# Loading k whole and first, then q by halves, for the first pair of heads of a bucketed attention with a rational feed-forward layer

## The chip, the cores and the metric

The kernel runs on 1 core of one Trainium2 chip. The metric is the device time of one execution in microseconds (us). The profile is of one execution; PE is TensorE (PEld its weight loads), DVE is VectorE, ACT is ScalarE, POOL is GpSimd, SP is SyncE, which here only issues transfers.

## The reference

Attention in which a query sees only the keys of its own bucket (six sign bits of a projection), then a feed-forward layer with a rational activation. Cut to what matters here:

```python
q_bits = (np.einsum('bhsd,dk->bhsk', q, proj) > 0).astype(np.int64)
k_bits = (np.einsum('bhsd,dk->bhsk', k, proj) > 0).astype(np.int64)
mask = q_bucket[:, :, :, None] == k_bucket[:, :, None, :]
scores = scale * np.matmul(q, k.transpose(0, 1, 3, 2))
scores = np.where(mask, scores, -1000000000.0)
scores = scores - np.max(scores, axis=-1, keepdims=True)
attn = np.exp(scores)
attn = attn / (np.sum(attn, axis=-1, keepdims=True) + 1e-09)
...
x = np.ascontiguousarray(attn_out.transpose(0, 2, 1, 3)).reshape(B * S, H * D)
h = x @ w_in
P = a[0] + a[1] * h + a[2] * h2 + a[3] * h3
Q = 1.0 + np.abs(b[0]) * np.abs(h) + np.abs(b[1]) * h2
return ((P / (Q + 1e-6)) @ w_out).astype(np.float32)
```

There are 4 batches of 8 heads, 768 tokens and 64 numbers per head; the layer has 3072 tokens, 512 by 2048 by 512.

## The kernel before, in words

The 32 heads are worked on as 16 pairs, numbered p. A pair's `qT[p]` and `kT[p]` are 128 by 768: one head's 64 rows above the other's, the tokens along the free dimension. Each operand is split into a high part of shorter format (`high`, a cast on ACT, tiles `q` and `k` of the profile) and a low part (`low`, a subtraction, tiles `lo`), and transfers and copies arrange high and low parts in `Q1`, `K1`, `Q2`, `K2`. Rows 64 and up of `Q1` and `K1` hold the bits of the buckets as penalties, so that one product gives the masked score.

For each pair, 12 steps of `maxstep` (two matmuls into `psm`, one DVE reduce to a column of `m`) find the maximum of each query row over all keys. The maxima go as a row into `Q1` (`shift_turn`, `shift_rows`; for pair 0 `first_shift`: three small matmuls into `pst`, then one DVE operation). Then 12 steps of `scores` (for each head two matmuls into `pss` and an exponential on ACT into `E`, with sums on POOL into `acc`) and 12 of `values` (`psv`). After the 16 pairs the layer runs, `psh` and `pso` in the profile.

Every engine executes in the order in which the program issues (lines 70 to 91), so an instruction that waits holds back all that stands behind it on its engine or queue. That order comes from a plan: `at(p, s, f)` (line 471) enters an action under the number 12p + s, and lines 582 to 584 issue them by rising number. The numbers in `FIRST` (lines 50 to 60) place the actions of pairs 0, 1 and 2; `MID` and `LAST` place the others. Before the plan comes a fixed list for pair 0 (lines 531 to 549).

Pair 0 has functions of its own, since nothing hides its start. `first_bits(t)` (line 294) projects q (t = 0) or k (t = 1) in two halves of 384 tokens into `psb_first`; `first_compare(t, hf)` (304) turns a half into bits on DVE; `first_penalties(h, hf)` (310) scales q's bits into `Q1` on ACT; `first_cross(t)` (314) copies the second head's rows down on ACT; `first_k_rows` (318) copies k's bit rows for the other head on POOL; `first_second_high` (321) makes four more copies on ACT; `second_low` (222) issues four transfers of the low parts on SP. `first_shift(hf, h)` (326) makes the row of maxima for one head and half. `warm(n)` (186) issues n matmuls on zeros, `psw`, whose result nobody reads. `maxstep` and `first_shift` share two PSUM buffers (`psa`).

The first actions of the plan, in order, are `maxstep` 0, 2, 1, 7, 6 of pair 0, `first_shift(0, 0)`, `maxstep` 8, two half `scores`, `first_compare(0, 1)`, `first_shift(0, 1)`, the bits of pair 1 (`second_bits`, `psb`, and two compares), four more half `scores`, and `maxstep` 4, 5, 9, 10. Steps 0 to 2 and 6 to 8 need only the first 384 tokens of q, but all of k.

Of the kernel before, what the change touches and what calls it, by code (L numbers as in the profile page):

```python
# [7 lines left out]
F32 = mybir.dt.float32  # L8
F32R = mybir.dt.float32r
# [4 lines left out]
ALU = mybir.AluOpType  # L14
# [4 lines left out]
P = 128  # L19
S = 768  # L20
HQ = 384
# [20 lines left out]
    group=6, values=[0.66, 0.05], values_out=3.5, maxima=7.17,  # L42
    maxima_steps=[0, 1.15, 1.73, 2.64, 3.32, 5.08, 5.86, 6.98, 8.0, 8.84, 10.26, 11.37], sums=14.65, sums_store=17.37,
    high=[-0.41, 1.19], low=[1.06, 3.35], bits=2.81, penalties=4.05, high_move=1.9, maskrows=5.61, second_low=-2.2,
    second_high=2.69, load_v=10.99, shift_turn=8.61, shift_rows=8.82, load=9.0, recips=[20.0, 22.0, 23.0],
    weights=[[1.44, 4.0, 4.1, 5.09, 5.49, 7.11, 9.5, 9.75, 17.5], [8.05, 10, 10.65, 11.5, 12.38, 14.29, 16.34, 19.32, 21.22]],
# [1 line left out]
)  # L48

FIRST = dict(  # L50
    maxima1=4.62, rate1=0.45, maxima2=9.5, rate2=0.82, high=[3.25, 3.53], low=[6.0, 7.3], bits=7.15, penalties=7.25,
    high_move=4.53, maskrows=8.2, second_low=4.25, second_high=4.35, load_v=4.78, group=2,
    values=[2.35, 2.65, 2.32, 2.35, 0.35, 0.61], values_out=3.02, high1=[-0.27, -5.58], low1=[11.24, 4.95],
    high_move1=20.05, load2=21.89, load3=-1.5, penalties1=-6.57, maskrows1=3.69,
    weights=[[-5.7, 6.64, 6.7, 11.42, 12.19, 18.75, 21.75, 38.77, 44.13], [8.03, 9.04, 9.24, 11.12, 14.81, 15.27, 15.99, 17.91, 46.81]],
    warm=6, warms=[3, 3, 3, 1, 1, 1], maxima00=[-4.26, -2.29, -4.17, 1.67, -1.15, 2.77], shift00=[2.15, 4.99],
    shift0=[3.67, 3.44], ahead=3, scores=[[3.68, 3.82, 7.26], [6.03, 8.25, 12.4]], pen01=[4.77, 14.55], comp01=3.35,
    second_high0=[-2.86, 2.12, -3.42, 3.45], load_v0=20.9, bits1=5.23, comp1=[15.82, 11.68],
    maxima0=[3.11, -1.97, -0.5, 2.14, 2.86, 3.25], turn1=[8.46, 13.26], rows1=[9.59, 14.35],
)  # L60

LAST = dict(
    group=6, values=[0.66, 0.19], values_out=0.98, vout14=0.94,
# [35 lines left out]
@with_exitstack  # L99
def bucket_attention_then_rational_ffn(ctx, tc, qT, kT, v, proj, w_in, w_out, coef, consts, out):  # L100
    nc = Ordered(tc)
    nc.scalar.preload_act_table_set("natural_log_exp_and_others")

    cpool = ctx.enter_context(tc.tile_pool(name="cpool", bufs=1))
    dpool = ctx.enter_context(tc.tile_pool(name="dpool", bufs=1, space=DRAM))
    wpool = ctx.enter_context(tc.tile_pool(name="wpool", bufs=1))


    raw = ctx.enter_context(tc.tile_pool(name="raw", bufs=4))
    ps_b = ctx.enter_context(tc.tile_pool(name="ps_b", bufs=1, space=PSUM))  # L110
    QF, KF = {}, {}

    def load(p, queue=nc.sync):
        for F, src, n in ((QF, qT, "q"), (KF, kT, "k")):
            F[p] = raw.tile([P, S], F32, tag="raw", name=f"{n}f{p}")
            queue.dma_start(F[p], src[p])

    load(0)
    prj = cpool.tile([P, 2, 32], F32, name="prj")
    nc.scalar.dma_start(prj, proj)  # L120
    cst = cpool.tile([P, 2 + P], F32, name="cst")
    nc.scalar.dma_start(cst, consts)
    ident = cst[:, 2 : 2 + P]
    load(1)
    ones = cpool.tile([P, 32], F32, name="ones")
    nc.vector.memset(ones, 1.0)
    ab = cpool.tile([P, 6], F32, name="ab")
    a0, a1, a2, a3, b0, b1 = (ab[:, i : i + 1] for i in range(6))
    absb1 = cpool.tile([P, 1], F32, name="absb1")
    qbias = cpool.tile([P, 1], F32, name="qbias")  # L130
    nc.vector.memset(qbias, 1.0 + 1e-6)

    x_d = [dpool.tile([P, S], F32, name=f"x_d{i}") for i in range(NPAIR)]
    s_d = [dpool.tile([2 * NHP, S], F32, name=f"s_d{i}") for i in range(B)]
    r_d = [dpool.tile([2 * NHP, S], F32, name=f"r_d{i}") for i in range(B)]

    wo_d = [dpool.tile([P, 2, DM], F32R, name=f"wo_d{i}") for i in range(NFC)]

    wi_hi = wpool.tile([P, NCC, DFF], F32R, name="wi_hi")
    wi_lo = wpool.tile([P, NCC, DFF], F32R, name="wi_lo")  # L140

    tokens = Tokens(tc, nc, raw, x_d, r_d)
    gemm = Gemm1(nc, ps_b, tokens, wi_hi, wi_lo)
    tail = ctx.enter_context(tc.tile_pool(name="tail", bufs=1))

    def coefficients():
        nc.sync.dma_start(ab, coef)
        yield
        nc.scalar.activation(absb1, b1, AF.Abs)
        yield  # L150

    early = ExitStack()
    right = ctx.enter_context(ExitStack())
    ffn = Ffn(tc, nc, tokens, gemm, wo_d, (a0, a1, a2, a3, b0, absb1, qbias), out)

    def operands_to_terms():
        early.close()
        ffn.terms_pool(right)

    last = attention(tc, nc, raw, ps_b, tail, tokens, early, operands_to_terms, ffn, load, QF, KF, v, w_in, w_out, wo_d, ident, cst,  # L160
                     ones, prj, wi_hi, wi_lo, x_d, s_d, r_d, coefficients)
    ffn.rest(ctx, last)
# [3 lines left out]
def attention(ctx, tc, nc, raw, ps_b, tail, tokens, early, operands_to_terms, ffn, load, QF, KF, v, w_in, w_out, wo_d, ident, cst, ones, prj,  # L166
# [5 lines left out]
    def operand(tag, p, shape, dtype, bufs=2):  # L172
        return opn[(NPAIR - 1 - p) % bufs == 0].tile(shape, dtype, tag=f"{tag}_{p % bufs}", name=f"{tag}_{p}")
# [12 lines left out]
    def warm(n):  # L186
        ps = ps_b.tile([P, 512], F32, tag="s", bufs=3, name=f"psw{len(WARM)}")
        WARM.append(n)
        for _ in range(n):
            nc.tensor.matmul(ps[:, 0:HQ], spare[:, 0:P], spare[:, P:512], start=True, stop=True)  # L190
# [8 lines left out]
    Q1, Q2, K1, K2, LO, V, M, MB, ACC, EXP, AV, MS = ({} for _ in range(12))  # L199
# [7 lines left out]
    def high(p, t):  # L207
        F, T, n = ((QF, Q1, "q"), (KF, K1, "k"))[t]
        if p not in T:
            T[p] = operand(f"{n}1", p, [P, 2, S], F32R, 3)  # L210
        nc.scalar.copy(T[p][:, t, :], F[p])
# [5 lines left out]
    def low(p, t, engine=nc.vector):  # L217
        F, T = ((QF, Q1), (KF, K1))[t]
        LO[p, t] = raw.tile([P, S], F32R, tag=f"lo{t}", name=f"lo{t}_{p}", bufs=1)
        engine.tensor_tensor(out=LO[p, t], in0=F[p], in1=T[p][:, t, :].bitcast(F32), op=ALU.subtract)  # L220

    def second_low(p):
        Q2[p] = operand("q2", p, [P, 2, S], F32R)
        K2[p] = operand("k2", p, [P, 2, S], F32R)
        for T, g in ((Q2[p], 0), (K2[p], 1)):
            move(nc, T[0:64, g, :], LO[p, g][0:64, :])
            move(nc, T[64:128, 1 - g, :], LO[p, g][64:128, :])

# [62 lines left out]

    def first_bits(t):
        if t == 0:
            mb = sm.tile([P, 2, HQ], F32R, tag="mb", name="mb0")
            MB[0], MB[1] = (mb, 0), (mb, 64)
        ps = MS[t] = ps_b.tile([P, 512], F32, tag="vs"[t], bufs=(1, 3)[t], name=f"psb_first{t}")
        F = (QF, KF)[t][0]
        for hf in range(2):  # L300
            o = 64 * hf + 32 * t
            nc.tensor.matmul(ps[o : o + 32, 0:HQ], prj[:, t, :], F[:, hf * HQ : hf * HQ + HQ], start=True, stop=True)

    def first_compare(t, hf):
        o = 64 * hf + 32 * t
        out = K1[0][64:96, 0, hf * HQ : hf * HQ + HQ] if t else MB[0][0][0:32, hf, :]
        nc.vector.tensor_scalar(out=out, in0=MS[t][o : o + 32, 0:HQ], scalar1=0.0, scalar2=cst[o : o + 32, 0:1],
                                op0=ALU.is_gt, op1=ALU.subtract)

    def first_penalties(h, hf):  # L310
        nc.scalar.activation(Q1[0][64:96, h, hf * HQ : hf * HQ + HQ], MB[0][0][0:32, hf, :].bitcast(F32), AF.Identity,
                             scale=hs[:, h : h + 1])

    def first_cross(t):
        F, T = ((QF, Q1), (KF, K1))[t]
        nc.scalar.copy(T[0][0:64, 1 - t, :], F[0][64:128])

    def first_k_rows():
        nc.gpsimd.tensor_copy(K1[0][64:97, 1, :], K1[0][64:97, 0, :].bitcast(F32))
# [197 lines left out]
    for i in range(2 * NFC):  # L517
        o = 12 * (i // 2)
# [9 lines left out]
        at(NPAIR - 1, x, ffn.step, f)  # L528
    at(NPAIR - 1, LAST["sums"], sums, NPAIR - 1)

    warm(12)
    K1[0] = operand("k1", 0, [P, 2, S], F32R, 3)
    nc.gpsimd.memset(K1[0][96:97, 0, :].bitcast(F32), 1.0)
    high(0, 0)
    first_bits(0)
    first_compare(0, 0)
    high(0, 1)
    first_bits(1)
    low(0, 0, nc.gpsimd)
    for hf in range(2):  # L540
        first_compare(1, hf)
    first_cross(1)
    low(0, 1, nc.gpsimd)
    first_penalties(0, 0)
    first_k_rows()
    second_low(0)
    first_cross(0)
    first_penalties(1, 0)
    warm(FIRST["warm"])
# [257 lines left out]
```

## Time and profile before

| | |
|---|---|
| time, median of 3 runs | 946.21 us (944.77 to 946.52) |
| the profiled execution's own time | 947.09 us |
| its span, first to last instruction | 945.3 us |
| PE busy | 936.1 us, 99% of the span |
| DVE busy | 868.7 us, 92% |
| ACT busy | 678.5 us, 72% |
| POOL busy | 445.1 us, 47% |
| mean granted TensorE clock | 0.997 |

A matmul is shown with a duration that overlaps the next one's, so the share of PE that is busy does not say that PE works at its peak: warm matmuls count in it as well. A row of the timeline merges neighbours of one kind: it gives the first start, the length of the whole, how many there are (x5), and in brackets how long the engine sat idle before and what ended that.

### The profile page before, as it was taken

How to read it: one execution, taken by the hardware profiler on the slowest of the kernel's cores; microseconds unless marked ns; L12 is line 12 of the kernel's file. 1: busy time of each engine (PE TensorE's matmuls, PEld its weight loads, DVE VectorE, ACT ScalarE, POOL GpSimd, SP SyncE). 2: the span in 40 equal slices, each digit the busy share in tenths (PEclk: the TensorE clock that was granted, in tenths of full speed). 3: DMA queues.
4: the chain of work that ended last, by engine and by line, in shares of the span. 5: the costliest groups of instructions: out<-in, count | busy, mean ns of one | idle time of the engine just before them, and what ended most of it. 6: DMA issues, size and time to landing. Idle time of an engine off the chain costs nothing.

```text
span 945.3 us, 14851 instructions
## 1 busy us (share of the span) xinstructions
PE 936.1 (99%) x5062; PEld 751.9 (80%) x5062; DVE 868.7 (92%) x1216; ACT 678.5 (72%) x1419; POOL 445.1 (47%) x395
## 2 busy tenths in 40 slices
PE   8999999999999999999999999999999999999997
PEld 4666666666666666589989989999899899899996
DVE  6799889888988896799999999999999999999996
ACT  7567767676767676687777777777777777777764
POOL 5587878787878787512222222222222222222222
PEclk9999999999999999999999999999999999999999
DMA  6677877778878778357021021021110110210000
GB/s 212 193 200 208 232 220 232 211 222 228 231 218 229 220 193 215 121 203 254 1 68 34 1 68 34 1 67 34 37 48 18 67 35 1 67 34 1 34 1 34
DMA packets 50032, 111.65 MB, mean 118 GB/s; under 512 B 9154, under 2 KB 22070, under 8 KB 49956
## 3 DMA queue, kind: packets, MB, share of 16 engines
q1 hardware_dynamic: 49524, 110.47, 39.4%
q8 instruction: 40, 0.66, 0.3%
q14 instruction: 36, 0.29, 0.1%
q10 hardware_dynamic: 432, 0.23, 0.1%
HBM read 56.82 MB, written 21.17 MB: 83 GB/s over the span
## 4 chain that ended last, share of the span: by engine, by line
PE 95%; DVE 3%; DMA 1%; ACT 0%; issue 0%; SPq 0%; ACTq 0%; DVEq 0%
PE psh L89 28%; PE pso L89 28%; PE pss L89 14%; PE psv L89 13%; PE psm L89 7%; PE psu L89 2%; DVE m L89 2%; PE psb L89 1%; DMA wr<-w_in 1%; DVE ws L89 1%; DMA kf<-kT 0%; PE pst L89 0%; ACT E L89 0%; DVE wr L89 0%; PE pst_None L89 0%
## 5 line engine op out<-in xcount | busy, mean ns | idle before, releaser
L89 POOL TENSOR_TENSOR gl<-c,gh 128x384 fp32r<-128x384 f32 x128 | 141.7, 1107 | 395.7 <-ACT gh L89 375.5
L89 ACT ACTIVATE E<-pss 128x384 f32<-128x384 f32 x384 | 167.6, 494 | 107.4 <-PE pss L89 93.7
L89 PE MATMUL pso<-wo,gh 128*128 128x512 f32 x768 | 240.5, 395 | 0.0
L89 DVE TENSOR_REDUCE m<-psm 128x1 f32<-128x768 f32 x192 | 179.6, 948 | 34.4 <-PE psm L89 30.8
L89 POOL TENSOR_TENSOR acc<-E,E 128x384 f32<-128x384 f32 x124 | 154.9, 1267 | 90.1 <-ACT E L89 89.9
L89 PE MATMUL pss<-q,k 128*128 128x384 f32 (+2 forms) x768 | 171.7, 347 | 1.4 <-ACT E L89 1.4
L89 PE MATMUL psh<-xl,wi_hi 128*128 128x384 f32 x512 | 172.1, 336 | 0.0
L89 PE MATMUL psh<-xh,wi_hi 128*128 128x384 f32 x512 | 171.7, 335 | 0.0
L89 PE MATMUL psh<-xh,wi_lo 128*128 128x384 f32 x512 | 171.5, 335 | 0.0
L89 PEld LDWEIGHTS pso<-wo,gh 128*128 128x128 f32 x768 | 142.8, 188 | 23.9
L89 PEld LDWEIGHTS pss<-q,k 128*128 128x128 f32 (+2 forms) x768 | 134.4, 189 | 30.7 <-issue 17.0
L89 ACT ACTIVATE h<-psh 128x384 f32<-128x384 f32 x128 | 63.1, 493 | 125.5 <-PE psh L89 125.4
L89 PE MATMUL pso<-wo,gl 128*128 128x512 f32 x384 | 151.3, 396 | 0.0
L89 DVE SCALAR_TENSOR_TENSOR c<-c,ab,r 128x384 f32<-128x384 f32 x128 | 147.0, 1149 | 0.0
L89 POOL TENSOR_TENSOR acc<-acc,E 128x384 f32<-128x384 f32 x124 | 138.3, 1134 | 4.3 <-ACT E L89 4.1
L89 PE MATMUL psv<-E,v 128*64 128x385 f32 x768 | 133.3, 496 | 0.0
L89 PEld LDWEIGHTS psv<-E,v 128*64 128x64 f32 x768 | 52.6, 138 | 66.6 <-issue 65.2
L89 PE MATMUL psm<-k,q 76*128 76x384 f32 (+1 forms) x384 | 102.0, 348 | 1.8 <-DVE m L89 1.0
L89 PEld LDWEIGHTS psh<-xh,wi_hi 128*128 128x128 f32 x512 | 96.1, 188 | 6.3 <-issue 1.2
L89 PEld LDWEIGHTS psh<-xl,wi_hi 128*128 128x128 f32 x512 | 96.0, 188 | 5.2
L89 PEld LDWEIGHTS psh<-xh,wi_lo 128*128 128x128 f32 x512 | 96.1, 188 | 0.0
L89 ACT ACTIVATE c<-psh,ab 128x384 f32<-128x384 f32 x128 | 86.5, 676 | 0.4 <-POOL gl L89 0.4
(81 smaller groups left out, 1289.5 us busy)
## 6 DMA issues: line engine op xcount, KB each, us to landing
q<-q SPq DMA_DIRECT2D x45, 192.0 KB
k<-k SPq DMA_DIRECT2D x45, 192.0 KB
wr<-w_in SPq DMA_DIRECT2D x16, 512.0 KB
wr<-w_out SPq DMA_DIRECT2D x16, 512.0 KB
wo_d<-wr SPq DMA_DIRECT2D x16, 512.0 KB
wo<-wo_d SPq DMA_DIRECT2D x16, 512.0 KB
qf<-qT SPq DMA_DIRECT2D x16, 384.0 KB
kf<-kT SPq DMA_DIRECT2D x16, 384.0 KB
```

The costliest lines, as they stand in the source:

```text
L89: return self.tc.keep_in_program_order(issue(*args, **kwargs))
```

## The change: k first, q by halves, and new numbers for the plan

The first load brings k whole, then q as two transfers of 384 tokens. The fixed list is put in another order; the bits, the high part and the low part of q are made by halves, the first half's low part on DVE. The first pair's `second_low` issues k's transfers ahead of q's. Fewer warm matmuls are issued (9 and 2 where 12 and 6 were). All numbers of `FIRST` change, and with them the order of the plan for pairs 0, 1 and 2.

```diff
+    maxima1=4.6, rate1=0.44, maxima2=9.46, rate2=0.83, high=[2.83, 1.95], low=[4.27, 6.05], bits=6.75, penalties=7.06,
+    high_move=3.75, maskrows=7.37, second_low=2.6, second_high=6.34, load_v=3.91, group=2,
+    values=[0.13, 2.57, 2.11, 2.3, 2.88, 1.99], values_out=3.29, high1=[2.25, -3.82], low1=[8.32, 2.23],
+    high_move1=22.05, load2=20.76, load3=0.03, penalties1=-1.25, maskrows1=1.3,
+    weights=[[-2.97, 6.62, 7.1, 11.65, 13.1, 13.55, 24.0, 50.79, 56.02], [6.95, 9.94, 10.22, 10.64, 13.59, 15.49, 15.99, 19.34, 36.58]],
+    warm=2, warms=[3, 3, 3, 1, 1, 1], maxima00=[-5.11, 0.96, -1.64, 3.86, 2.67, 3.53], shift00=[2.46, 5.11],
+    shift0=[3.05, 4.21], ahead=3, scores=[[3.75, 4.24, 10.63], [5.75, 6.32, 15.48]], pen01=[4.17, 17.42],
+    comp01=-0.89, second_high0=[-1.44, 0.27, -0.46, 1.65], load_v0=15.61, bits1=5.63, comp1=[13.21, 9.98],
+    maxima0=[2.25, 1.02, 0.25, 3.0, 3.78, 2.48], turn1=[7.74, 12.92], rows1=[8.08, 13.05], warm0=9,
...
-    load(0)
+    KF[0] = raw.tile([P, S], F32, tag="raw", name="kf0")
+    nc.sync.dma_start(KF[0], kT[0])
+    QF[0] = raw.tile([P, S], F32, tag="raw", name="qf0")
+    for hf in range(2):
+        nc.sync.dma_start(QF[0][:, hf * HQ : hf * HQ + HQ], qT[0][:, hf * HQ : hf * HQ + HQ])
...
-        for T, g in ((Q2[p], 0), (K2[p], 1)):
+        for T, g in ((Q2[p], 0), (K2[p], 1))[:: -1 if p == 0 else 1]:
...
+    def first_high(hf):
...
+        nc.scalar.copy(Q1[0][:, 0, qs], QF[0][:, qs])
+
+    def first_low(hf, engine):
...
+        engine.tensor_tensor(out=LO[0, 0][:, qs], in0=QF[0][:, qs], in1=Q1[0][:, 0, qs].bitcast(F32), op=ALU.subtract)
...
-    warm(12)
+    warm(FIRST["warm0"])
     K1[0] = operand("k1", 0, [P, 2, S], F32R, 3)
     nc.gpsimd.memset(K1[0][96:97, 0, :].bitcast(F32), 1.0)
-    high(0, 0)
-    first_bits(0)
+    first_cross(1)
+    first_bits(1)
+    first_compare(1, 0)
+    high(0, 1)
+    low(0, 1, nc.gpsimd)
+    first_high(0)
+    first_bits(0, (0,))
     first_compare(0, 0)
-    high(0, 1)
-    first_bits(1)
-    low(0, 0, nc.gpsimd)
-    for hf in range(2):
-        first_compare(1, hf)
-    first_cross(1)
-    low(0, 1, nc.gpsimd)
+    first_low(0, nc.vector)
+    first_compare(1, 1)
     first_penalties(0, 0)
+    first_bits(0, (1,))
+    first_high(1)
+    first_low(1, nc.gpsimd)
     first_k_rows()
     second_low(0)
     first_cross(0)
```

By the new numbers the plan begins `maxstep` 0, 2, `first_compare(0, 1)`, `maxstep` 1, `first_shift(0, 0)`, `maxstep` 7, 8, a half `scores`, `maxstep` 6, a half `scores`, `first_shift(0, 1)`, `second_bits`, four half `scores`, `maxstep` 5, 4, then `values` 0 and 1 (eight `psv` matmuls), `maxstep` 3, 11, `scores` 3, `maxstep` 9, `first_shift(1, 0)`, `maxstep` 10, `scores` 4, `first_shift(1, 1)`, and `maxstep` 0 of pair 1. On SP `load_v(0)` and `load(2)` come ahead of the first transfer of `w_in` and of `high_move(1)`; they came behind both.

## Rows read from the trace of the kernel before

**Rows 1.** Busy time by stretch: length, busy us (instructions), clock, DMA share, GB/s.
```profile
core 0: us, PE busy (x) PEld busy (x) DVE busy (x) ACT busy (x) POOL busy (x), PEclk, DMA share, GB/s
16.90:27.00 10.10, 9.06 (x51) 6.17 (x50) 7.67 (x10) 5.88 (x11) 5.99 (x5) 1.00 0.54 172
27.00:48.00 21.00, 20.86 (x117) 12.72 (x115) 16.10 (x20) 11.25 (x24) 13.96 (x13) 1.00 0.73 200
48.00:60.00 12.00, 12.00 (x73) 8.15 (x75) 12.00 (x16) 8.36 (x20) 9.90 (x8) 1.00 0.87 207
```

**Rows 2.** The chain that ended last, 0 to 60 us: start, length, what.
```profile
1.18 4.48 DMA kf<-kT
```

**Rows 3.** Timeline of ACT from 3 to 17 us.
```profile
4.16 0.83 ACT L89 CAST q<-qf 128x768 fp32r<-128x768 f32 x1 [2.15 <-DMA qf<-qT]
5.69 1.69 ACT L89 CAST k<-kf 128x768 fp32r<-128x768 f32 x2 [0.69 <-DMA kf<-kT]
7.40 0.61 ACT L89 ACTIVATE q<-mb,hs 32x384 fp32r<-32x384 f32 x1
```

**Rows 4.** Timeline of PE, 0 to 17 us.
```profile
8.06 0.62 PE L89 MATMUL psm<-k,q 96*128 96x384 f32 x2 [0.43 <-ACT q L89]
...
12.32 0.82 PE L89 MATMUL pst<-cst,m 128*1 128x128 f32 x6
...
14.77 0.82 PE L89 MATMUL pst<-cst,m 128*1 128x128 f32 x6
```

**Rows 5.** Timeline of DVE, 0 to 20 us.
```profile
5.92 0.60 DVE L89 TENSOR_SCALAR mb<-psb_first,cst 32x384 fp32r<-32x384 f32 x1 [4.57 <-PE psb_first L89]
6.59 1.27 DVE L89 TENSOR_SCALAR k<-psb_first,cst 32x384 fp32r<-32x384 f32 x2
8.72 4.42 DVE L89 TENSOR_REDUCE m<-psm 128x1 f32<-128x768 f32 x5 [0.85 <-PE psm L89]
13.25 0.56 DVE L89 TENSOR_SCALAR q<-pst 1x384 fp32r<-1x384 f32 x1
...
14.84 0.61 DVE L89 TENSOR_SCALAR mb<-psb_first,cst 32x384 fp32r<-32x384 f32 x1
15.63 0.56 DVE L89 TENSOR_SCALAR q<-pst 1x384 fp32r<-1x384 f32 x1 [0.18 <-PE pst L89]
```

**Rows 6.** Timeline of POOL, 0 to 9 us.
```profile
5.13 1.82 POOL L89 TENSOR_TENSOR lo<-qf,q 128x768 fp32r<-128x768 f32 x1 [3.31 <-ACT q L89]
```

**Rows 7.** Timeline of the SP queue, 0 to 20 us.
```profile
8.76 1.11 SPq L89 DMA_DIRECT2D k<-lo  x2
```

**Rows 8.** Timelines of POOL and DVE, 44 to 62 us.
```profile
45.19 1.98 POOL L89 TENSOR_TENSOR acc<-E,E 128x384 f32<-128x384 f32 x2 [5.06 <-ACT E L89]
...
50.62 2.71 POOL L89 TENSOR_TENSOR acc<-E,E 128x384 f32<-128x384 f32 x2 [0.71 <-ACT E L89]
...
46.45 1.27 DVE L89 SCALAR_TENSOR_TENSOR ws<-ws,wr 128x512 int32<-128x512 int32 x1
...
48.50 0.68 DVE L89 SCALAR_TENSOR_TENSOR ws<-ws,wr 128x512 int32<-128x512 int32 x1
...
51.44 1.01 DVE L89 TENSOR_TENSOR lo<-qf,q 128x768 fp32r<-128x768 f32 x1
```

**Rows 9.** Costliest group with a 128x384 cast on ACT, whole span: busy us, mean ns.
```profile
L89 ACT CAST gh<-c 128x384 fp32r<-128x384 f32 x128 | 63.8, 498 | 3.6 <-DVE c L89 3.6
```

**Rows 10.** Timeline of PE, 18 to 31 us.
```profile
18.58 0.87 PE L89 MATMUL psm<-k,q 96*128 96x384 f32 x4
20.23 0.59 PE L89 MATMUL psm<-k,q 96*128 96x384 f32 x2 [0.79 <-DVE m L89]
...
23.29 1.51 PE L89 MATMUL psv<-E,v 128*64 128x385 f32 x8
...
26.95 0.51 PE L89 MATMUL psm<-k,q 76*128 76x384 f32 x2
```

**Rows 11.** Groups of PE by form, 27 to 60 us: busy us, mean ns.
```profile
L89 PE MATMUL psm<-k,q 76*128 76x384 f32 x44 | 12.2, 367 | 0.1
```

More of the change, by code (lines that the diff above doesn't have):

```diff
@@ L50 @@
 FIRST = dict(
[L51 to L59, printed above, removed]
+    maxima1=4.6, rate1=0.44, maxima2=9.46, rate2=0.83, high=[2.83, 1.95], low=[4.27, 6.05], bits=6.75, penalties=7.06,
[7 more added lines that the diff above has]
+    maxima0=[2.25, 1.02, 0.25, 3.0, 3.78, 2.48], turn1=[7.74, 12.92], rows1=[8.08, 13.05], warm0=9,
 )
@@ L290, in shift_rows, with first_bits @@
                 move(nc, Q1[p][76:77, h, hf * HQ : hf * HQ + HQ].rearrange("o (i c) -> o i c", c=P), src[3 * h : 3 * h + 3, :])
-    def first_bits(t):
-        if t == 0:
+    def first_bits(t, halves=(0, 1)):
+        if t == 1:
             mb = sm.tile([P, 2, HQ], F32R, tag="mb", name="mb0")
             MB[0], MB[1] = (mb, 0), (mb, 64)
-        ps = MS[t] = ps_b.tile([P, 512], F32, tag="vs"[t], bufs=(1, 3)[t], name=f"psb_first{t}")
+        tag = "s" if t or halves[0] else "v"
+        ps = ps_b.tile([P, 512], F32, tag=tag, bufs=3 if tag == "s" else 1, name=f"psb_first{t}_{halves[0]}")
         F = (QF, KF)[t][0]
-        for hf in range(2):
+        for hf in halves:
+            MS[t, hf] = ps
             o = 64 * hf + 32 * t
@@ L306, in first_compare @@
         out = K1[0][64:96, 0, hf * HQ : hf * HQ + HQ] if t else MB[0][0][0:32, hf, :]
-        nc.vector.tensor_scalar(out=out, in0=MS[t][o : o + 32, 0:HQ], scalar1=0.0, scalar2=cst[o : o + 32, 0:1],
+        nc.vector.tensor_scalar(out=out, in0=MS[t, hf][o : o + 32, 0:HQ], scalar1=0.0, scalar2=cst[o : o + 32, 0:1],
                                 op0=ALU.is_gt, op1=ALU.subtract)
@@ L316, in first_cross @@
         nc.scalar.copy(T[0][0:64, 1 - t, :], F[0][64:128])
+    def first_high(hf):
+        if hf == 0:
+            Q1[0] = operand("q1", 0, [P, 2, S], F32R, 3)
+        qs = slice(hf * HQ, hf * HQ + HQ)
+        nc.scalar.copy(Q1[0][:, 0, qs], QF[0][:, qs])
+    def first_low(hf, engine):
+        if hf == 0:
+            LO[0, 0] = raw.tile([P, S], F32R, tag="lo0", name="lo0_0", bufs=1)
+        qs = slice(hf * HQ, hf * HQ + HQ)
+        engine.tensor_tensor(out=LO[0, 0][:, qs], in0=QF[0][:, qs], in1=Q1[0][:, 0, qs].bitcast(F32), op=ALU.subtract)
     def first_k_rows():
@@ L529, in attention @@
     at(NPAIR - 1, LAST["sums"], sums, NPAIR - 1)
-    warm(12)
+    warm(FIRST["warm0"])
     K1[0] = operand("k1", 0, [P, 2, S], F32R, 3)
     nc.gpsimd.memset(K1[0][96:97, 0, :].bitcast(F32), 1.0)
-    high(0, 0)
-    first_bits(0)
-    first_compare(0, 0)
-    high(0, 1)
-    first_bits(1)
-    low(0, 0, nc.gpsimd)
-    for hf in range(2):
-        first_compare(1, hf)
-    first_cross(1)
-    low(0, 1, nc.gpsimd)
+    first_cross(1)
[5 more added lines that the diff above has]
+    first_bits(0, (0,))
+    first_compare(0, 0)
+    first_low(0, nc.vector)
+    first_compare(1, 1)
     first_penalties(0, 0)
+    first_bits(0, (1,))
+    first_high(1)
+    first_low(1, nc.gpsimd)
     first_k_rows()
```

## The prediction

> **What bounds the kernel now.** I read the busy time by stretch first, because it bounds what a change to the first pair can touch. From 27 us on TensorE stands idle for 0.14 us in 21 and then not at all, while from 16.9 to 27 us it is busy for 9.06 of 10.10 us [rows 1]. So the kernel is bound by TensorE's queue, and the change is worth what it adds to or takes from TensorE's lost time before about 27 us, plus small waits up to 60 us, where the renumbered actions end. The chain of waits comes next: it starts with the landing of k, 1.18 + 4.48 = 5.66 us [rows 2], and the timelines of the engines show what follows. ACT casts q from 4.16 us, waits for k, does two k casts up to 7.38 us and the penalties up to 8.01 us [rows 3]; the first product of the maxima starts at 8.06 us, released by ACT [rows 4], and the first reduce at 8.72 us [rows 5]. From there to 15 us DVE hardly pauses: five reduces end at 13.14 us, the row of maxima follows at 13.25 us, and the second row at 15.63 us waits 0.18 us [rows 5].
>
> **The first reduce.** k now has the place of q in the queue and lands when q did, 4.16 us [rows 3]. ACT then copies k across (0.83 us) and casts k (0.84 us, half of 1.69) [rows 3], to 5.85 us. k's low part on POOL follows: in the row of before POOL started 0.13 us after ACT's cast ended (5.13 against 4.16 + 0.84) and took 1.82 us [rows 6], so it holds POOL from 5.98 to 7.80 us. Meanwhile DVE does a compare of k and one of q, about 0.65 us each with the step to the next [rows 5], and ACT casts the first half of q by 6.4 us (0.50 us, a cast of this shape [rows 9]). The compares need the constants, whose landing no row shows; it lies by 5.92 us, the first compare of before [rows 5], so the pair of compares ends between 6.4 and 7.2 us. Then stands q's first low part on DVE, a subtraction with both inputs in SBUF.
>
> Such an operation of DVE does not run beside one of POOL in these rows. Two additions on POOL take 1.98 us, and 2.71 us where a DVE subtraction of 1.01 us falls among them; a DVE operation of 0.68 us takes 1.27 us when it starts at 46.45 us, before POOL's pair of 45.19 + 1.98 = 47.17 us has ended, and ends 0.55 us after it [rows 8]. So q's low part on DVE waits for POOL, to 7.80 us, and then takes half of 1.01 us [rows 8]: 8.30 us. The page "SBUF — State Buffer" of the Trainium skill (section "SBUF: two separate sides") says the same as a rule: VectorE and GpSimd share one pair of ports, and whichever starts first keeps it for the whole instruction. By that rule the sum is the one here; if the two engines ran side by side, all that follows would come 0.6 to 0.7 us earlier, and these rows agree with the rule.
>
> Behind the waiting subtraction stands the compare of k's second half, which TensorE needs for the second matmul of the first product: 8.30 + 0.04 + 0.63 (half of 1.27) = 8.97 us. Before, the product led from 8.06 us to a reduce at 8.72 us, 0.66 us [rows 4, 5]; now its first matmul has been done by then, and I estimate what is left at 0.38 us (the two matmuls that the row shows with 0.62 us start some 0.28 us apart). So the first reduce starts at 8.97 + 0.05 + 0.38 = 9.40 us, **0.68 us later** than before. The bounds: 0.1 us earlier without the wait, 0.7 later with it; I take the later one, as the rows show the wait. That k comes first earns nothing here.
>
> **The rows of maxima.** In the new order `first_shift(0, 0)` stands right behind the reduce of `maxstep` 1 on DVE. It needs three transposing products after that reduce, and their row before took 13.25 - 12.32 = 0.93 us from the first product to DVE's start [rows 4, 5]; with 0.05 us to reach TensorE, DVE pauses 0.98 us. Before, the products ran behind two more reduces, and the pause was 13.25 - 13.14 = 0.11 us. **Cost 0.87 us.** `first_shift(0, 1)` now stands right behind the reduce of `maxstep` 6 and pauses 0.98 us again. Before, the compare of q's second half (14.84 to 15.45 us) filled that gap and only 0.18 us was left [rows 5]; the compare now runs on its own ahead of `maxstep` 1, 0.65 us. **Cost 0.98 + 0.65 - 0.18 - 0.65 = 0.80 us**, the 0.65 being the same work in both. Nothing else on DVE lies there to hide either. TensorE's order ties the rest to it: the bits of pair 1 and eight score matmuls follow the second row, so `maxstep` 5 starts 0.68 + 0.87 + 0.80 = 2.35 us later than its counterpart, at about 20.93 instead of 18.58 us [rows 10].
>
> **What comes back.** Before, TensorE waited 0.79 us for DVE at 20.23 us [rows 10]. Now eight value products (1.44 us to the next start [rows 10]) stand there. From the start of `maxstep` 5 the longest chain is then DVE's: 0.6 us to the first reduce (0.66 us at 8.06 us [rows 4, 5]), reduces 5 and 4 (0.88 us each), 0.5 us until the values have passed and product 3 is there, reduces 3, 11 and 9 (2.7), a row of maxima (0.65), reduce 10 (0.95), and the products of the other row (0.82 [rows 4]). That is 8.0 us to the first product of pair 1, against 26.95 - 18.58 = 8.37 us before: **0.35 us back** (bounds 0 and 0.79). Between 27 and 60 us the gain can only come from product pairs that wait for a reduce: a pair takes 0.62 us where it waits and 0.51 where it doesn't [rows 4, 10], 0.11 us for at most 22 pairs [rows 11], so 0 to 2.4 us. I take **0.8 us**, a third, as values, weights and bits are spread more evenly but most pairs still follow a reduce.
>
> **What costs nothing.** The loads: one more transfer on SP delays pair 1's loads by 0.4 us, and they are needed by ACT at 9 us or later. k's low parts go out first, q's about 9.7 us, against 9.87 us for the last of before [rows 7]; the first scores come 4 us later, which hides this. `load_v`, `load(2)` and `w_in` change places on SP ahead of `high_move(1)`, which waits for ACT at 14 us anyway; `load(3)` waits for POOL's low part of pair 1, which stands earlier now. One ACT cast more (0.17 us of overhead) lies beside DVE's pauses. Fewer warm matmuls are no work saved, since nothing waits for them; but TensorE then stands nearly idle up to 9 us, longer than the 0.43 us of before [rows 4]. The granted clock is 1.00 in every stretch of rows 1; were it half up to 12 us, three pairs would each take 0.36 us more, under a reduce's 0.88 us (4.42 over 5 [rows 5]). I take 0, with 0.5 us as the upper end.
>
> **The sum.** 2.35 - 0.35 - 0.8 = +1.2 us. The profiled execution took 947.09 us, so 948.3 us by it; it lies 0.88 us above the median of the runs, and against that the forecast is **947.4 us**. 0.2% is 1.9 us, about what a measurement of this kernel can tell from no change, so the forecast is a small loss inside that bound.
>
> **The rivals.** *Forecast* (0.42): 946.5 to 948.1 us, +0.3 to +1.9.
>
> *All of the delay stays* (0.32), the slower side: DVE reaches pair 1 2.35 us late, and since each product pair waits for a reduce, TensorE's queue stays late. 946.21 + 2.35 = 948.6 us, and 949.1 with the clock's 0.5. For it: only 0.14 us of idle time after 27 us [rows 1]. Against: the 0.79 us. It decides if less than 0.45 us has been won back by 60 us.
>
> *DVE's order doesn't bind* (0.13): the two pauses hide behind TensorE's own work. Then +0.68 - 0.35 - 0.8 = -0.5, 945.7 us. Against: before, TensorE filled this stretch with warm matmuls.
>
> *It is faster* (0.13): the subtraction doesn't wait, so the first reduce comes at 8.6 us; the pauses hide; and all of the 2.4 us between 27 and 60 us are won: -0.1 - 0.35 - 2.4, some 943.4 us, or 944.2 if two thirds of it are.
>
> **How the numbers follow.** The likeliest case gives 947.4 us. The range is 944.6 to 949.4: the upper end is the slower rival's 949.1 and the 0.3 us by which the highest run of before lies over the median; the lower end takes in the third case with as much below it as the bounds of what comes back leave (1.1 us), and leaves out most of the last. Faster by over 0.2% is the last rival and the tail of the third, 0.14; slower is the second rival and a tail of the forecast, 0.34; the rest, 0.52, is within 0.2%.
>
> **What would show it.** Right: k's first cast at 4.2 us; q's subtraction on DVE shown with about 1.2 us or more, ending with POOL's; the first reduce near 9.4 us; about 0.95 us of idle DVE ahead of both rows of maxima; pair 1's first product near 29 us against 26.95. Wrong: a first reduce ahead of 8.7 us, a short subtraction beside POOL's, rows of maxima without a pause, or pair 1's first product before 27.5 us.

## The result and the profile after

The change makes the kernel slower, by a little: a median of 948.24 us over 10 runs (946.64 to 949.67) against 946.04 us over 10 runs of the kernel before. The ratio is 1.0022, with an interval of 1.0012 to 1.0032, so +1.1 to +3.0 us. The forecast was +1.2 us, and the rival in which all of the delay stays was +2.35 us. The time lies between the two, nearer to the rival and 0.1 us above the upper end of the forecast's own case (948.1 us). The interval holds both, so the median does not decide between them.

The profiled execution took 948.24 us, with a span of 946.4 us. TensorE is busy for 934.8 us, DVE for 866.8 us; both shares are what they were. The difference has to be read from the start, and there DVE's timeline of the kernel after, 5 to 30 us, answers to [rows 5].

```profile
5.97 0.61 DVE L89 TENSOR_SCALAR k<-psb_first,cst 32x384 fp32r<-32x384 f32 x1 [4.62 <-PE psb_first L89]
6.62 0.60 DVE L89 TENSOR_SCALAR mb<-psb_first,cst 32x384 fp32r<-32x384 f32 x1
7.15 1.02 DVE L89 TENSOR_TENSOR lo<-qf,q 128x384 fp32r<-128x384 f32 x1
8.21 0.62 DVE L89 TENSOR_SCALAR k<-psb_first,cst 32x384 fp32r<-32x384 f32 x1
9.53 1.82 DVE L89 TENSOR_REDUCE m<-psm 128x1 f32<-128x768 f32 x2 [0.70 <-PE psm L89]
...
13.68 0.56 DVE L89 TENSOR_SCALAR q<-pst 1x384 fp32r<-1x384 f32 x1 [0.69 <-PE pst L89]
14.27 2.69 DVE L89 TENSOR_REDUCE m<-psm 128x1 f32<-128x768 f32 x3
17.87 0.56 DVE L89 TENSOR_SCALAR q<-pst 1x384 fp32r<-1x384 f32 x1 [0.91 <-PE pst L89]
...
21.25 1.82 DVE L89 TENSOR_REDUCE m<-psm 128x1 f32<-128x768 f32 x2 [0.93 <-PE psm L89]
```

Three things are to be seen. The subtraction `lo<-qf,q` begins at 7.15 us and ends at 8.17 us. The first reduce starts at 9.53 us, before at 8.72. And both rows of maxima (`q<-pst`) have a pause in brackets, 0.69 and 0.91 us, where before the first row shows none and the second 0.18 [rows 5].

POOL's timeline of the kernel after, 0 to 14 us, shows what the subtraction stood beside:

```profile
5.96 1.80 POOL L89 TENSOR_TENSOR lo<-kf,k 128x768 fp32r<-128x768 f32 x1 [4.14 <-ACT k L89]
```

POOL's ends at 7.76 us, DVE's 0.41 us later. ACT's timeline of the kernel after, 0 to 18 us, answers to [rows 3]:

```profile
4.15 1.67 ACT L89 CAST k<-kf 64x768 fp32r<-64x768 f32 x2 [2.13 <-DMA kf<-kT]
5.73 0.51 ACT L89 CAST q<-qf 128x384 fp32r<-128x384 f32 x1
8.21 0.61 ACT L89 ACTIVATE q<-mb,hs 32x384 fp32r<-32x384 f32 x1 [1.98 <-DVE lo L89]
```

k does land when q did, and k's cast and q's first half are done by 6.24 us. Then ACT stands idle for 1.98 us and is released by the subtraction: the penalties go into the rows of `Q1` from which the subtraction still reads. This wait the prediction did not have. The chain of waits of the kernel after, 0 to 30 us, goes through it (start, length, what):

```profile
7.22 0.96 DVE lo L89
8.19 0.02 issue
8.21 0.62 ACT q L89
8.83 0.04 issue
8.88 0.63 PE psm L89 x2
9.51 0.02 issue
9.53 1.83 DVE m L89 x2
```

TensorE's timeline of the kernel after, over the first 75 us, answers to [rows 4] and [rows 10]; its last line is the first score product of pair 2, behind pair 1's twelve steps of the same form:

```profile
8.88 0.62 PE L89 MATMUL psm<-k,q 96*128 96x384 f32 x2 [1.55 <-ACT q L89]
...
13.04 0.60 PE L89 MATMUL pst<-cst,m 128*1 128x128 f32 x4 [1.01 <-DVE m L89]
...
17.01 0.49 PE L89 MATMUL pst<-cst,m 128*1 128x128 f32 x3 [0.57 <-DVE m L89]
...
20.70 0.86 PE L89 MATMUL psm<-k,q 96*128 96x384 f32 x4
21.50 1.51 PE L89 MATMUL psv<-E,v 128*64 128x385 f32 x8
...
28.52 0.62 PE L89 MATMUL psm<-k,q 76*128 76x384 f32 x2
...
74.53 0.97 PE L89 MATMUL pss<-q,k 77*128 77x384 f32 x4
```

The same line of the kernel before:

```profile
72.91 0.97 PE L89 MATMUL pss<-q,k 77*128 77x384 f32 x4
```

Against before, the kernel after is late by 0.81 us at the first reduce, 2.12 at `maxstep` 5 (20.70 against 18.58, where `maxstep` 4 had this place), 1.57 at pair 1's first product (28.52 against 26.95) and 1.62 at pair 2's first score. So nothing was won between 27 and 75 us. Two stretches of equal work show it, from that first product to that first score: length, then TensorE's busy time and matmuls. Before:

```profile
26.95:72.91 45.96, 45.72 (x259) 29.60 (x258) 40.79 (x49) 28.46 (x63) 34.51 (x30) 1.00 0.75 204
```

After:

```profile
28.52:74.53 46.01, 45.62 (x258) 29.47 (x258) 41.56 (x50) 27.48 (x61) 33.61 (x30) 1.00 0.72 202
```

TensorE has the same matmuls (one record fewer) and is idle for 0.24 us in one and 0.39 us in the other. The 58 matmuls of `maxstep` that lie in each take 365 ns on average before and 363 after, so about as many pairs waited for a reduce as before. The new order of this work took nothing off its length.

### The profile page after: what moved, and what is told of

It is laid out like the page before. It is cut to its first block, busy times and chain, and to the rows that moved or that the text cites. A ratio compares the mean times of both kernels' runs of the same rounds, so it can differ in the third digit from the quotient of the medians.

```text
span 946.4 us, 14838 instructions
## 1 busy us (share of the span) xinstructions
PE 934.8 (99%) x5055; PEld 750.5 (79%) x5055; DVE 866.8 (92%) x1217; ACT 679.5 (72%) x1420; POOL 441.9 (47%) x395
## 4 chain that ended last, share of the span: by engine, by line
PE 92%; DVE 3%; DMA 2%; SPq 1%; ACT 1%; issue 1%; POOL 0%; ACTq 0%; DVEq 0%; POOLq 0%
PE pso L89 28%; PE psh L89 28%; PE pss L89 13%; PE psv L89 12%; PE psm L89 7%; PE psu L89 2%; DMA wr<-w_in 2%; DVE m L89 2%; PE psb L89 1%; SPq L89 1%; DVE ws L89 0%; DMA k<-mb 0%; ACT E L89 0%; DVE wr L89 0%; PE psw L89 0%
## 5 line engine op out<-in xcount | busy, mean ns | idle before, releaser
L89 POOL TENSOR_TENSOR acc<-acc,E 128x384 f32<-128x384 f32 x124 | 136.3, 1119 | 7.9 <-ACT E L89 7.7
```

Source lines behind the costliest of these rows:

```text
L89: return self.tc.keep_in_program_order(issue(*args, **kwargs))
```

## The experiments

The times differ by 2.4 us at most and each execution has small disturbances of its own, so each verdict rests first on three marks of the profile, told as us later than in the kernel before: its first reduce (8.72 us), pair 1's first product (26.95 us) and pair 2's first score (72.91 us). The expectations on record speak in part of pair 1's first score. That proved a poor mark, since the new plan puts eight value matmuls behind it that came ahead of it before (the kernel after is late by only 0.38 us there). Each mark is read from one execution. The last two rows of the table are the same kernel, and they lie 0.64 to 0.70 us apart at every mark, while the step from the first mark to the second agrees within 0.06 us; so the steps between marks say more than a mark alone.

| kernel | first reduce | pair 1's first product | pair 2's first score | ratio to before, 95% |
|---|---|---|---|---|
| after | +0.81 | +1.57 | +1.62 | 1.0022 (1.0012 to 1.0032) |
| new_head_old_plan | +0.71 | +0.66 | +0.69 | 1.0015 (1.0005 to 1.0026) |
| old_head_new_plan | +0.43 | +1.26 | +1.34 | 1.0014 (0.9997 to 1.0030) |
| low_before_port_is_taken | +0.50 | +1.27 | +1.30 | 1.0008 (0.9998 to 1.0018) |
| low_on_pool_first | -0.25 | +0.62 | +0.72 | 1.0012 (1.0003 to 1.0022) |
| rows_covered | +0.67 | +2.66 | +2.72 | 1.0025 (1.0014 to 1.0037) |
| covered_old_head | +0.17 | +0.66 | +0.73 | 1.0015 (1.0003 to 1.0026) |
| rows_and_scores_moved | +0.71 | +0.17 | +0.30 | 1.0012 (0.9999 to 1.0025) |
| more_warm | +0.66 | +1.43 | +1.50 | 1.0014 (1.0005 to 1.0024) |
| best_guess | +0.08 | +0.56 | +0.65 | 1.0006 (0.9997 to 1.0015) |
| pool_head_old_plan | -0.20 | -0.24 | -0.61 | 0.9994 (0.9982 to 1.0006) |
| pool_head_rows_scores | -0.67 | -1.19 | -1.18 | 0.9996 (0.9986 to 1.0007) |
| the same, once more | -0.03 | -0.49 | -0.50 | 1.0000 (0.9991 to 1.0009) |

**The two halves of the change.** One kernel has the new fixed list with the old numbers of `FIRST`, the other the old list with the new numbers.

```diff
 new_head_old_plan, from the kernel after
-    warm=2, warms=[3, 3, 3, 1, 1, 1], maxima00=[-5.11, 0.96, -1.64, 3.86, 2.67, 3.53], shift00=[2.46, 5.11],
+    warm=2, warms=[3, 3, 3, 1, 1, 1], maxima00=[-4.26, -2.29, -4.17, 1.67, -1.15, 2.77], shift00=[2.15, 4.99],
...
 old_head_new_plan, from the kernel before
-    warm=6, warms=[3, 3, 3, 1, 1, 1], maxima00=[-4.26, -2.29, -4.17, 1.67, -1.15, 2.77], shift00=[2.15, 4.99],
+    warm=2, warms=[3, 3, 3, 1, 1, 1], maxima00=[-5.11, 0.96, -1.64, 3.86, 2.67, 3.53], shift00=[2.46, 5.11],
...
```

> The changed kernel with k first and the new fixed list, but with the plan's numbers of before (9 and 2 warm matmuls kept). My theory: the new list costs 0.8 us at the first reduce (9.53 against 8.72 us) whatever the plan; the plan of before adds no pauses ahead of the rows of maxima, so the four reduces after pair 1's bits start about 0.8 us later than in before (20.0 against 19.13 us), and the scores of pair 1 start 0.5 to 0.8 us later: a time of +0.5 to +0.9 us against before. Rival one (the plan's order alone makes the loss, the list does not matter): within 0.2 us of before at the scores of pair 1. Rival two (list and plan fit each other only together): later than the changed kernel, +2 us or more.

> The kernel before with its loads and its fixed list, but with the plan's new numbers (12 warm matmuls first, 2 after the list). My theory: first reduce at 8.7 us as before; DVE pauses 0.7 to 1.0 us ahead of both rows of maxima, so the reduces after pair 1's bits start 1.3 us later than before (20.4 us), and the scores of pair 1 about 0.8 us later: a time of +0.6 to +1.0 us against before. Rival one (the plan's order makes the whole loss): +1.6 us at the scores of pair 1. Rival two (the pauses are hidden, the list makes the loss): within 0.3 us of before.

With the old plan, the list's delay of 0.71 us goes through unchanged: +0.66, then +0.69. DVE's subtraction in new_head_old_plan, and POOL's:

```profile
6.59 1.48 DVE L89 TENSOR_TENSOR lo<-qf,q 128x384 fp32r<-128x384 f32 x1
...
5.86 1.81 POOL L89 TENSOR_TENSOR lo<-kf,k 128x768 fp32r<-128x768 f32 x1 [4.04 <-ACT k L89]
```

It starts 0.56 us earlier than in the kernel after, is shown 0.46 us longer, and again ends 0.4 us behind POOL's (8.07 against 7.67). The ratio, +1.4 us with an interval from +0.5 to +2.5, is above the +0.5 to +0.9 us expected, but its interval holds them.

The plan alone: the first reduce is late by 0.43 us, which was not expected. DVE's timeline of old_head_new_plan, and TensorE's:

```profile
7.35 1.27 DVE L89 TENSOR_SCALAR k<-psb_first,cst 32x384 fp32r<-32x384 f32 x2
...
8.11 1.01 PE L89 MATMUL psm<-k,q 96*128 96x384 f32 x2 [0.91 <-ACT q L89]
```

DVE's compares of k end at 8.62 us, against 6.59 + 1.27 = 7.86 us before [rows 5], and the second matmul of the first product, at 8.67 us, waits for them; so the two are shown with 1.01 us in place of 0.62, at a granted clock of 1.00. The compares are late because TensorE finished q's projections later than before (the first compare starts at 6.71 us, against 5.92), and no edit lies ahead of these projections. So this is a difference between executions: covered_old_head, with the same list, has its first reduce at 8.89 us.

From the first reduce to the reduces behind pair 1's bits it takes 20.94 - 9.15 = 11.79 us, against 19.13 - 8.72 = 10.41 before. The rows of maxima in old_head_new_plan, DVE's timeline:

```profile
13.37 0.56 DVE L89 TENSOR_SCALAR q<-pst 1x384 fp32r<-1x384 f32 x1 [0.76 <-PE pst L89]
...
17.55 0.56 DVE L89 TENSOR_SCALAR q<-pst 1x384 fp32r<-1x384 f32 x1 [0.91 <-PE pst L89]
```

The two pauses come with the plan, whatever the list. Of their 1.38 us, 0.55 are back by pair 1's first product, where +1.26 is left.

**The subtraction's place.** Either it goes ahead of POOL's on DVE, or the half goes to POOL ahead of k's.

```diff
 low_before_port_is_taken, from the kernel after
     first_bits(1)
+    first_high(0)
+    first_low(0, nc.vector)
     first_compare(1, 0)
     high(0, 1)
     low(0, 1, nc.gpsimd)
-    first_high(0)
     first_bits(0, (0,))
     first_compare(0, 0)
-    first_low(0, nc.vector)
...
 low_on_pool_first, from the kernel after
     first_compare(1, 0)
-    high(0, 1)
-    low(0, 1, nc.gpsimd)
     first_high(0)
+    first_low(0, nc.gpsimd)
     first_bits(0, (0,))
     first_compare(0, 0)
-    first_low(0, nc.vector)
     first_compare(1, 1)
+    high(0, 1)
+    low(0, 1, nc.gpsimd)
```

> The changed kernel with ACT's first half of q cast ahead of k's second cast, and q's first low part first on DVE, ahead of the compares, so that it runs before POOL takes k's low part. My theory: the subtraction takes 0.4 to 0.5 us instead of 1.02, and the penalties, which overwrite rows that it reads, wait for the compare alone; the first reduce starts at 8.5 to 8.9 us instead of 9.53, and the scores of pair 1 come 0.6 to 1.0 us earlier than in the changed kernel (+0.6 to +1.0 us against before). Rival (the wait for POOL does not set the first reduce, the landing of q or of the constants does): first reduce within 0.2 us of 9.53 us and the time of the changed kernel.

> The changed kernel with q's first low part on POOL, ahead of k's, and ACT's cast of that half ahead of k's second cast; DVE only compares. My theory (the order on the shared port and the penalties that overwrite what the subtraction reads set the first product): the subtraction takes 1.0 us on POOL from 6.0 to 7.0 us, the penalties follow, the first reduce starts at 8.3 to 8.6 us instead of 9.53, and with the plan's pauses kept the scores of pair 1 start at +0.5 to +0.8 us against before. Rival (the three compares or the landings set it): first reduce at 9.1 us or later.

In low_before_port_is_taken DVE's subtraction runs before POOL's, which starts at 6.80 us:

```profile
5.96 0.56 DVE L89 TENSOR_TENSOR lo<-qf,q 128x384 fp32r<-128x384 f32 x1 [4.61 <-ACT q L89]
```

It takes 0.56 us instead of 1.02 to 1.68, so the wait for POOL is shown. The first reduce gained only 0.31 us (9.22), less than expected: the three compares now stand behind it in series and end at 8.46 us, and the penalties wait for the second of them. In low_on_pool_first DVE has only compares, and the first reduce comes 1.06 us ahead of the kernel after and 0.25 us ahead of before:

```profile
8.47 1.82 DVE L89 TENSOR_REDUCE m<-psm 128x1 f32<-128x768 f32 x2 [0.77 <-PE psm L89]
```

That is as expected, and so is +0.72 at pair 2's first score: the list costs nothing any more, the plan's cost is left.

**The two rows.** `rows_covered` gives the first row of maxima and the compare of q's second half later numbers, so that two reduces stand between the first row's last maximum and the row, and the compare stands ahead of the second row; `covered_old_head` does the same under the old list. Then `rows_and_scores_moved` also moves a half score.

```diff
 rows_covered and covered_old_head: the first three; rows_and_scores_moved: all four
-    shift00=[2.46, 5.11]
+    shift00=[3.6, 5.11]
-    pen01=[4.17, 17.42]
+    pen01=[4.6, 17.42]
-    comp01=-0.89
+    comp01=4.5
-    scores=[[3.75, 4.24, 10.63], ...]
+    scores=[[3.9, 4.24, 10.63], ...]
```

> The changed kernel with the first row of maxima moved behind the reduces of steps 7 and 8, and the compare of q's second half moved between the last of the six reduces and the second row, as it stood before. My theory: first reduce at 9.53 us as in the changed kernel; the pauses ahead of the rows fall from 0.69 and 0.91 us (and 0.61 us of compare ahead) to 0.2 us or less each; the reduces after pair 1's bits start 1.2 to 1.6 us earlier than in the changed kernel (19.7 to 20.0 against 21.25 us). At the scores of pair 1 this is worth 0.6 to 1.2 us, so +0.5 to +1.0 us against before. Rival (TensorE's own queue sets the pace there and the pauses are hidden): the scores of pair 1 start within 0.2 us of the changed kernel's, +1.6 us against before.

> The old loads and fixed list with the new plan, in which the first row of maxima stands behind the reduces of steps 7 and 8 and the compare of q's second half between the last reduce and the second row. My theory: from the first reduce to the reduces after pair 1's bits it takes 10.4 us, as in the kernel before (10.41), and not 11.8 as with the uncovered rows; the new plan wins back 0.5 us after that, so the scores of pair 1 start 0 to 0.5 us earlier than in before: a time within 0.5 us of before or up to 0.5 us below it. Rival (the pauses are not what the new plan costs): 11.5 us or more between these two points, and +0.8 us or more at the scores of pair 1.

> The changed kernel with the covered rows as before, and the first half score moved behind the product of step 6, because in the covered run with the old list that score waited 0.73 us for the row of maxima in TensorE's queue and held back the product behind it. My theory: now no pause over 0.3 us is left ahead of the rows or the sixth reduce; from the first reduce to the reduces after pair 1's bits 10.4 to 10.6 us instead of 11.72; the scores of pair 1 start about 1.2 us earlier than in the changed kernel, if what the new plan wins back later (0.5 us) stays: at +0.2 to +0.6 us against before for a first reduce near 9.4 us. Rival (what the plan wins back later is only the making up of its own pauses): no more than 10.6 us between the points, but +0.7 us or more at the scores of pair 1.

In the profiled execution of rows_covered TensorE had been idle for 1.71 us ahead of its first product, and the granted clock fell right behind it. The stretch of 9 to 13 us, with TensorE's clock in the third column from the end:

```profile
9.00:13.00 4.00, 4.00 (x16) 2.35 (x15) 2.28 (x3) 3.89 (x6) 3.12 (x3) 0.57 0.74 186
```

TensorE's timeline shows the price, a pair of matmuls in 1.09 us where 0.65 is usual:

```profile
8.74 0.62 PE L89 MATMUL psm<-k,q 96*128 96x384 f32 x2 [1.71 <-ACT q L89]
...
9.87 1.09 PE L89 MATMUL psm<-k,q 96*128 96x384 f32 x2
```

The reduces behind pair 1's bits came at 22.34 us, 12.95 us after the first, so this run says nothing of the pauses. Its ratio, +2.4 us, shows no gain either, where +0.5 to +1.0 us was expected. In covered_old_head they took 11.45 us, where 10.4 was expected: the first pause was gone, but a new one stood behind the row. TensorE's timeline of that kernel, and DVE's:

```profile
14.04 0.62 PE L89 MATMUL pss<-q,k 97*128 97x384 f32 x2 [0.73 <-DVE q L89]
...
15.05 0.96 DVE L89 TENSOR_REDUCE m<-psm 128x1 f32<-128x768 f32 x1 [1.06 <-PE psm L89]
```

The half score needs the row, waits for it at the head of TensorE's queue, and holds back the product of `maxstep` 6. With the half score behind that product, in rows_and_scores_moved, DVE's timeline has no such pause:

```profile
9.43 4.42 DVE L89 TENSOR_REDUCE m<-psm 128x1 f32<-128x768 f32 x5 [0.70 <-PE psm L89]
13.89 0.56 DVE L89 TENSOR_SCALAR q<-pst 1x384 fp32r<-1x384 f32 x1
14.56 0.96 DVE L89 TENSOR_REDUCE m<-psm 128x1 f32<-128x768 f32 x1
16.43 0.56 DVE L89 TENSOR_SCALAR q<-pst 1x384 fp32r<-1x384 f32 x1 [0.27 <-PE pst L89]
19.83 1.82 DVE L89 TENSOR_REDUCE m<-psm 128x1 f32<-128x768 f32 x2 [0.95 <-PE psm L89]
```

19.83 - 9.43 = 10.40 us, as with the old plan. So four numbers of the plan are the whole of the two pauses, 11.72 - 10.40 = 1.32 us, and at pair 2's first score the kernel gains 1.62 - 0.30 = 1.32 us on the kernel after. The ratio, 1.0012 with an interval from 0.9999, does not show it.

**More warm matmuls.** 10 instead of 2 stand ahead of the first product.

```diff
-    warm=2
+    warm=10
```

> The changed kernel with 10 warm matmuls instead of 2 ahead of the first product (no other edit). Theory: besides its queue order the changed kernel loses in some executions because TensorE is nearly idle for 1.5 us ahead of the first product and its clock falls to half after 9 us, as in the run with the covered rows; with the gap filled the profile shows the clock at 1.0 up to 100 us, the highest times go, and the median falls by 0.3 to 0.6 us against the changed kernel (to +1.3 to +1.9 us against before). Rival (the clock in the first 20 us costs nothing, DVE sets the pace): the median stays at +1.9 to +2.5 us against before.

The marks and the ratio are those of the kernel after within their spread: inconclusive. The profiled executions of the kernel after, with 2, and of this one show no fall of the clock at the start, so nothing was there to win in them.

**The edits together.** `best_guess` has POOL's list, the first three numbers and 7 warm matmuls. `pool_head_rows_scores` has POOL's list and all four numbers, and ran once more under a second name; `pool_head_old_plan` has POOL's list with the old numbers. Each is a union of the edits shown above.

> The three together: q's first low part on POOL first, the covered rows of maxima, 7 warm matmuls ahead of the first product. If the parts add: first reduce at 8.3 to 8.6 us, 10.4 us to the reduces after pair 1's bits, 0.5 us won back after, so the scores of pair 1 start 0.5 to 1.0 us earlier than in before: 0.5 to 1.0 us below before. If they do not add (rival): at or above before.

> The same two moves in the kernel that makes q's first low part on POOL first (2 warm matmuls). My theory, with parts that add: first reduce at 8.3 to 8.5 us, 10.4 to 10.6 us to the reduces after pair 1's bits, the scores of pair 1 0.3 to 0.9 us earlier than in before, a time 0.3 to 0.9 us below before's. Rival (winning back is only the making up of its own pauses): the scores of pair 1 within 0.3 us of before's.

> The loads and the list with q's first low part on POOL first, and the plan's numbers of before. My theory: first reduce at 8.3 to 8.5 us, 10.4 us to the reduces after pair 1's bits as in the kernel before, nothing won back later, so the scores of pair 1 start 0.2 to 0.4 us earlier than in before. Rival (what follows waits for something else than the first reduce, a transfer or ACT): no earlier than in before.

> The same kernel as in the run with q's first low part on POOL first and rows and score moved, once more, with nothing changed. If the gain up to pair 1 is the kernel's own: first reduce at 8.0 to 8.5 us, scores of pair 1 0.7 to 1.2 us earlier than in before. If the slips between 190 and 265 us of the first look (weights of w_in that landed late) are chance, the time is 0.5 to 1.2 us below before's; if this order of transfers brings them about, they come again at the same places and the time is before's.

In best_guess the pause moved behind the row as in covered_old_head, and its 7 warm matmuls stood ahead of the first product: the first reduce came at 8.80 us against 8.47 in low_on_pool_first. So these parts did not add, as its rival had it. The other two are ahead of before at pair 2's first score, by 0.5 to 1.2 us, yet their ratios neither show nor exclude a gain of that size, and the repeated run did not improve on the first. In the profiled execution of the repeated run the 0.50 us are lost again on the way to 200 us, and then ACT waits. ACT's timeline, before:

```profile
200.24 0.67 ACT L89 ACTIVATE ws<-wr 128x512 f32<-128x512 f32 x1 [0.37 <-DMA wr<-w_in]
```

And in pool_head_rows_scores_again:

```profile
204.08 0.68 ACT L89 ACTIVATE ws<-wr 128x512 f32<-128x512 f32 x1 [4.07 <-DMA wr<-w_in]
```

SP issued this transfer of `w_in` at 193.16 us before and at 193.68 us here, so the transfer is late, not its issue. ACT waits at this place in all thirteen other profiled executions, for 0.83 to 4.07 us; in before for 0.37. In pool_head_rows_scores the wait is 3.77 us, so it came again in the repeated run, as the last expectation has it for an order of transfers that brings it about. But new_head_old_plan and pool_head_old_plan, which issue by the old plan, wait 3.34 and 2.37 us, so the new plan's order is not needed for it. No run edits that order by itself, and the cause stays open.

## Why the prediction was right and wrong

**The first reduce: right, by a mechanism with one part missing.** Forecast 9.40 us, measured 9.53. The subtraction did wait for POOL's, in every kernel that kept it there, and took 0.56 us where it did not. Forecast was 8.30 us for its end, measured 8.17. The missing part is ACT's penalties, which wait for the same subtraction and ended at 8.82 us, level with the compare (8.83 us). So both led to the product at 8.88 us. That the sum came within 0.13 us is in part luck. It had the first matmul of this product done ahead of the compare's end and 0.43 us left behind that; neither matmul had begun, and it took 0.70 us from 8.83 us to the reduce. Against that, the compare ended 0.14 us earlier than forecast.

**The rows of maxima: right in place, somewhat too dear.** Forecast 0.87 + 0.80 = 1.67 us, measured 11.72 - 10.41 = 1.31. The first pause was 0.69 us, not 0.98: TensorE had done one of the row's three products already, and only four matmuls were left to wait for the maximum (`pst`, x4 at 13.04 us). The delay at `maxstep` 5 was 2.12 us where 2.35 was forecast.

**What comes back by pair 1: right, and more.** Forecast 0.35 us, measured 2.12 - 1.57 = 0.55.

**What comes back between 27 and 60 us: this step failed.** The forecast took 0.8 us, a third of a bound of 2.4 us, without a row that shows fewer pairs waiting; it measured 1.57 - 1.62 = -0.05. The bound counted 0.11 us for each of 22 product pairs that might wait for a reduce [rows 11], but the same rows give the mean of the 44 matmuls of these pairs as 367 ns before, and the same row of the kernel after, 27 to 60 us, gives 364 ns:

```profile
L89 PE MATMUL psm<-k,q 76*128 76x384 f32 x44 | 12.1, 364 | 0.3 <-DVE m L89 0.2
```

So the new order spares 44 x 3 ns, 0.1 us: the pairs wait for their reduces as they did. In eleven of the twelve runs the second and third marks of the table differ by 0.13 us or less; only pool_head_old_plan won 0.37 us there, and it has the plan of before, so that no new order did it. So the sum is 2.12 - 0.55 + 0.05 = +1.62 us by the trace where +1.2 was forecast. The rival's condition, less than 0.45 us back by 60 us, was all but met: 0.50 us came back.

**What the median has beyond that.** +2.2 us against +1.62 at pair 2's first score. The interval of the ratio, +1.1 to +3.0 us, holds 1.62, so the 0.6 us need no cause of their own. Behind 75 us the two profiled executions drift apart in both directions. By the first matmul of each pair's sums (`psu`) the kernel after is 1.62 us late at 76 us, 1.78 at 219, 2.79 at 266 and 1.11 from 385 us on, where the spans end too; the step down is at 377 to 384 us, where TensorE's granted clock is 0.77 in the kernel before and 1.00 in the kernel after. Between 171 and 266 us the eleven profiled executions with k loaded first lost 0.5 to 8.0 us against before, the two with the old loads and list 0.4 at most. But the medians do not follow: pool_head_old_plan lost 1.7 us there, and its ratio is 0.9994. No run settles which of this belongs to the change.

**What costs nothing.** The loads and the fewer warm matmuls cost nothing in the profiled execution of the kernel after: no wait for them there, and clock 1.00. The upper end set for the clock, 0.5 us, was too low: in rows_covered, with the clock at 0.57, the stretch to the reduces behind pair 1's bits took 12.95 us, 1.50 us more than the 11.45 of covered_old_head, which has the same plan and kept 1.00.

**The parts add up.** The second mark less the first is what the plan does by itself. With the old numbers it is -0.05 and -0.04 us; with the new ones +0.76 to +0.87 in five kernels of the table; with three edits +0.48 and +0.49 (rows_covered, with its fallen clock, is left out); with all four -0.46 to -0.54. So the change is 0.8 to 0.9 us from the plan and some 0.7 from the list, and by the marks each can be undone alone. The list's share is the less certain: the five executions with its subtraction behind POOL's have their first reduce at 9.38 to 9.53 us, but the three with the old list at 8.72 (before), 8.89 and 9.15 us, so against the mean of these it costs 0.5 us. Without its pauses the new plan is 0.5 us better by these marks than the old one; that this shortens the kernel was not shown.

## What to carry to other kernels

A delay at a kernel's start need not melt away. Here it stayed over the next 46 us, in which the engine that bounds them was idle for 0.24 us and its products waited as often as before; look for such time before counting on it. An operation that needs a reduce's result at once pauses its engine; here two reduces or a compare in between took most of the pause away. Whatever needs that operation's result must move too, or the pause only changes place. Work given to DVE to spare POOL gained nothing here, since it could not run beside POOL's: all that waited behind it paid for POOL's work.

## What the runs showed of the hardware

The wait between DVE and POOL is sharp: DVE's subtraction was shown with 1.02, 1.48 and 1.68 us as it started at 7.15, 6.59 and 6.39 us, and ended at 8.07 to 8.17 us each time, some 0.4 us behind POOL's. The duration shown contains the wait, so a long row need not be a slow operation.

TensorE's clock at the start differs from execution to execution. In rows_covered it was granted at 0.57 from 9 to 13 us, so for most of that time at the lower of its two levels (1.2 of 2.4 GHz), after 1.71 us of idle time. The kernel after idled for 1.55 us at the same place, and new_head_old_plan for longer than rows_covered; both kept 1.00, so the length of this idle time does not settle it:

```profile
8.78 0.62 PE L89 MATMUL psm<-k,q 96*128 96x384 f32 x2 [1.88 <-ACT q L89]
```

The landing of q differs too. In the two executions of pool_head_rows_scores the first reduce came at 8.05 and 8.69 us; in the later one the second half of q landed at 6.99 us, and its projections stood ahead of the first product on TensorE. A difference of half a microsecond at the first reduce therefore says little from one profile.

A transfer of 512-column weights in the middle of the kernel landed 10.4 us after its issue in one kernel and 7 us after it in the kernel before, with nothing edited near it. ACT, in order, waited for 4.07 us, more than the 2.2 us of the whole change.
